# Softmax row sums in half as many matmuls, the first x tiles transposed by TensorE, and four PSUM banks for the first dense layer, in a gated mix of recurrent attention and an MLP

## The chip, the cores and the metric

The kernel runs on 1 core of one Trainium2 chip. The metric is the device time of one execution in microseconds (us); the figure of a kernel is the median of its runs. A granted TensorE clock of 1 means full speed.

## The reference

x is 2048 tokens of 512 numbers in bfloat16. The result is `g * a + (1 - g) * b`, with a gate g of one number per token.

```
g = sigmoid((x * gate_w).sum(-1, keepdims=True))
# a: recurrent attention, 64 segments of 32 tokens, M = 8 memory rows, 32 heads of 128
for s in range(n_seg):
    h = concatenate([mem, xs], axis=1)                 # 40 rows of 512
    q, k, v = h Wq, h Wk, h Wv                         # per head
    scores = where(mask, q k^T * Dh ** -0.5, -1e9)     # memory rows see all; tokens are causal
    p = softmax(scores, axis=-1)
    o = (p v) summed over heads through Wo
    mem = o[:, :M]                                     # goes into the next segment
    outs.append(o[:, M:])
# b: a token-wise MLP, F = 1376
y = (x - mean) / sqrt(var + 1e-5)
b = gelu(y w1 + b1) w2 + b2
```

The memory makes the 64 segments a chain: segment s+1 needs the eight memory rows that segment s put out.

## The kernel before

**Order of the work.** All of it stands in an order written out by hand (a manual schedule): each engine runs its instructions in the order in which the Python code issues them, and waits at each for its inputs and for its output tile to be free. There are no planner and no priorities. The eight PSUM banks are fixed: U[0] to U[3], X1, X2, SbF and W, all of 512 float32 columns.

**Start and MLP stage.** SyncE (SP) issues most loads, ScalarE (ACT) x tile 1 and the first piece of w2, GpSimd (POOL) the bias b1 and the broadcast of gate_w (L344). Eleven matmuls on the identity (`warm`, L524 to 528) run on TensorE (PE) while the first x tiles land. The 16 tiles of 128 tokens are worked off in 8 blocks of two. `prep` normalises a block's tiles on VectorE (DVE), `prep_tr` (L455) transposes them by PE through X1 and X2. `a_mm` (L477) is the first dense layer: for each of 11 chunks fc of the hidden size, four matmuls of 256 columns into a bank, then a Gelu on ScalarE (L483) that empties the bank. The bank (L480) goes by turns through SbF and W in blocks 1 to 6; the first four chunks of all and the last block use others. `b_mm` (L485) is the second dense layer for the same block, two chunks behind, into U[0] to U[3]. For nine of the tiles (DEF) it is put off: their hidden values go to DRAM (`spill`), and the loop computes them later in halves of four 256-column matmuls into W (`mlp_halves`, L667), one `next(mlp)` each, with the values fetched back by SP (`hm_load`). `gate_sums` (L462) multiplies x by gate_w on VectorE, and `gates` (L467) takes the tanh on ScalarE. At block 3, SP loads tiles 0 and 1 of x in transposed form (`load_xT`, L100, from L358) for the recurrent loop.

**One step of the loop** (L753 to 866, s from 0 to 63; each is one segment, T and si are its tile of 128 tokens and its place in it). Small matmuls are laid out four at a time in the PE array's four 32-wide column groups (`tile_position`), one per group of heads. In order:

- Q and K: 64 matmuls of 512 columns into U[0], U[2], U[1], U[3] (`qk_unit`, L125); ScalarE casts each bank to Tb (L133), VectorE transposes Tb into QT or KT (L137).
- `scores(s, 0)` (L261): 16 matmuls of 40 columns and four of 64, on top of a mask in SbF, for heads 0 to 15. The columns of a group of four heads are 8 left-over token keys' queries, then 32 queries (8 to 40), then two pieces of 8 for the memory rows (40 to 48, and 48 to 56 for the left-over keys), 56 in all (EW). ScalarE takes the exponential into E (L805).
- V: `v_unit(X1, ...)` four times, and one of the four for X2 (L147). ScalarE casts to V (L811).
- Sums over keys for heads 0 to 15, by matmuls with a block matrix of ones BO. `xsums` (L697) makes those of the 32 token columns: eight matmuls (four for columns 8 to 40, four for 0 to 8 that add to them), E as the weights, four columns of BO moving, into SbF[:, 224:232]. `msum` (L796, by `sums`, L275) makes those of the memory rows: four matmuls of 32 columns into U[1][:, 320:352], then four more that add the left-over keys' columns. `mnorm` (L799): VectorE takes the reciprocal (L801) from U[1] into SbF[:, 288:320], then multiplies it into E (L802).
- `scores(s, 1)` in U[0] for heads 16 to 31, two exponentials (first the memory columns 40 to 56, then the rest), two more V units.
- One MLP half, then `msum(1)` into U[3] and `mnorm(1)` through the SBUF tile RS; the last V unit, two V casts.
- Fill work (left-over tokens of the next tile and the like), one MLP half, `xsums(E, 1)`, and `recip_x` (L710): reciprocal of the 8 columns of sums into R; R to DRAM (r_dr, 4 KB) and back, broadcast to all partitions as Rb (512 KB), both by SP; copies of the memory rows' reciprocals into R; the mask written afresh into SbF with zeros for the next sums (`mask_put`, L257); POOL adds R into racc.
- `av` (L283): E times V, in two halves i2 = 0 and 1, into U[0] to U[3]; the memory columns of E are normalised by now, the token columns aren't. ScalarE casts the memory columns to UT (L842), the raw token columns to XR (L707).
- The output projection `wo_pass` (L732) into X2 with UT, which holds this step's memory rows and the token rows of step s-1; casts to w; `new_mem` (L740) puts the eight memory rows into the next step's input hT, by PE and VectorE.
- `x_norm(s)` (L725) runs on POOL at the start of step s+1: it multiplies XR by Rb, which arranges the reciprocals by head and query, into the next UT and into UL (L730, four instructions).

racc and rmin gather all reciprocals; at the end they decide whether a slower, safe version of the attention (tc.If) has to run. It doesn't here.

Of the kernel before, what the change touches and what calls it, by code (L numbers as in the profile page):

```python
# [28 lines left out]
def kernel(ctx, tc, A_x, A_mem0, A_Wq, A_Wk, A_Wv, A_Wo, A_seg_len, B_x, B_w1, B_b1, B_w2, B_b2, gate_w, out):  # L29
# [50 lines left out]

    MkF = ep.tile([P, 4 * EW + NG + 2 * M], BF16)
    Mk = MkF[:, 0:4 * EW].rearrange("p (a c) -> p a c", c=EW)
# [170 lines left out]
    RS = ep.tile([P, 32], FP32)  # L253
    RP = [SbF[:, 288:320], RS[:]]


    def mask_put(i2):  # L257
        c = 4 * EW + (NG + 2 * M if i2 == 0 else 0)
        nc.vector.tensor_copy(out=(SbF, U[0])[i2][:, 0:c], in_=MkF[:, 0:c])
# [41 lines left out]
    with tc.tile_pool(name="mlpw", bufs=1) as mlpw, \  # L301
# [129 lines left out]
        def prep(blk):  # L431
# [3 lines left out]
            for tt in range(TB):  # L435
# [3 lines left out]
                if blk == 0:  # L439
                    nc.vector.tensor_scalar(out=ve[:, tt:tt + 1], in0=mv[:, tt, 1:2], scalar1=LN_EPS, scalar2=None, op0=ALU.add)  # L440
                    nc.scalar.activation(out=rs[:, tt:tt + 1], in_=ve[:, tt:tt + 1], func=ACTF.Sqrt)
            if blk == 0:
                nc.scalar.activation(out=dummy[:], in_=ident[:, 0:1], func=ACTF.Gelu_apprx_tanh)
            else:
                nc.vector.tensor_scalar(out=ve[:], in0=mv[:, :, 1], scalar1=LN_EPS, scalar2=1.0 / (RSQRT_K * RSQRT_K), op0=ALU.add, op1=ALU.mult)
                rsqrt(rs[:], ve[:], TB)
# [80 lines left out]

        warm(NWARM)
        prep(0)
# [66 lines left out]
    UL = [cw.tile([P, 4, NG, 32], BF16, tag=f"UL{i}", bufs=1, name=f"UL{i}") for i in range(2)]  # L596
    racc = lp.tile([P, NG * 40], FP32)
    rmin = lp.tile([P, NG * 40], FP32)
# [93 lines left out]

    xs8 = SbF[:, 4 * EW:4 * EW + NG]
    xs8z = SbF[:, 4 * EW + NG:4 * EW + NG + 2 * M]
    RW = 9 * NG

    def xsums(E, h):  # L697

        for c0, n in ((8, 32), (0, LEFT)):
            for c in range(4):  # L700
                nc.tensor.matmul(xs8[32 * c:32 * c + n, 4 * h:4 * h + 4], lhsT=E[:, 4 * h + c, c0:c0 + n], rhs=BO[:, 0:P:32],  # L701
                                 start=False, stop=True, skip_group_check=True, tile_position=(0, 32 * c))

# [6 lines left out]
    def recip_x(s):  # L710
        R = Rs.pop(s)
        nc.vector.reciprocal(out=R[:, 8 * NG:RW], in_=xs8)
# [12 lines left out]
    def x_norm(s):  # L725
        T, si = divmod(s, SPT)
        XR, Rb = XRs.pop(s), Rbs.pop(s)[:].rearrange("p (c q) (h j) -> p h j c q", c=4, h=2)
        for out, o, a, b in ((UT[(s + 1) % 2], M, LEFT, 32), (UL[T % 2], LEFT * si, 0, LEFT)):
            for h in range(2):
                nc.gpsimd.tensor_tensor(out=out[:, :, 4 * h:4 * h + 4, o:o + b - a], in0=XR[:, :, 4 * h:4 * h + 4, a:b], in1=Rb[:, h, :, :, a:b], op=ALU.mult)  # L730

# [21 lines left out]
    for s in range(nseg):  # L753
# [42 lines left out]
        def msum(i2):  # L796
            sums(U[1 + 2 * i2][:, 320:352].rearrange("p (i q) -> p i q", q=8), E[:, 4 * i2:4 * i2 + 4, :], 40, 48, 8, True)

        def mnorm(i2):  # L799
            r, e = RP[i2], E[:, 4 * i2:4 * i2 + 4, 40:56].rearrange("p i (a q) -> p i a q", q=8)  # L800
            nc.vector.reciprocal(out=r, in_=U[1 + 2 * i2][:, 320:352])  # L801
            nc.vector.tensor_tensor(out=e, in0=e, in1=r.rearrange("p (i q) -> p i q", q=8).unsqueeze(2).to_broadcast([P, 4, 2, 8]), op=ALU.mult)  # L802
# [22 lines left out]
        if not last:  # L825
            if s:
                next(mlp, None)
            msum(1)
# [231 lines left out]
```

## Time and profile before

| | before |
|---|---|
| median of 3 runs | 751.95 us (751.55 to 753.9) |
| the profiled execution | 755.67 us, its span 753.8 us |
| granted TensorE clock | 0.998 |
| PE busy | 736.0 us (98%), 19896 matmuls |
| ACT busy | 535.6 us (71%) |
| DVE busy | 399.5 us (53%) |
| POOL busy | 274.2 us (36%) |
| DMA traffic | 77.17 MB, of which Rb 63 times 512 KB |
| last first-layer matmuls | from 68.75 us |
| Q and K of step 0 | from 74.58 us |

The profile is one execution, taken by the hardware. Names are those of the program with buffer numbers left out, so U stands for U[0] to U[3] and X for X1 and X2. A row of a group gives the line, the engine, the operation, `out<-in` and the count; then the busy time in us and the mean of one in ns; then the idle time just before them and who ended it. A row of the timeline starts with its start and duration in us, and shows in brackets the idle time before it and who ended that. "x8" in it are eight instructions in one row; its duration is from the first one's start to the last one's modelled end. Matmuls are pipelined, so ends overlap: what PE spends on a row is the distance to the start of the next one. "issue" is time in which an engine waited for nothing that the profile shows. A step of the loop takes some 10.5 us (the multiply from RS comes 63 times from 80.9 to 730.4).

### The profile page before, as it was taken

The numbers are of one execution on the slowest core, as the hardware profiler recorded it, in microseconds if no ns is written. First come the engines' busy times: TensorE is split into PE (matmuls) and PEld (weight loads), VectorE is DVE, ScalarE is ACT, GpSimd is POOL, SyncE is SP. The second block draws the span as 40 slices with busy tenths as digits, with TensorE's granted clock in tenths as the row PEclk, the third lists the DMA queues.
The fourth block names the chain that finished last, engine by engine and source line by source line (L and its number), as shares of the span: only waits on it lengthen the run. The fifth ranks groups of instructions, "written<-read, shape, count | busy, mean of one in ns | idle before, by whom it ended". The sixth has DMA issues, their size and how long they took to land.

```text
span 753.8 us, 45384 instructions
## 1 busy us (share of the span) xinstructions
PE 736.0 (98%) x19896; PEld 429.8 (57%) x19896; DVE 399.5 (53%) x1415; ACT 535.6 (71%) x1627; POOL 274.2 (36%) x516
## 2 busy tenths in 40 slices
PE   8999999999999999999999999999999999999996
PEld 5776555555555555555555565555555655555553
DVE  6776555446454554445554545445464545555444
ACT  5777667777776776777777777767777777777663
POOL 4001323444324444334433344333443334433341
PEclk9999999999999999999999999999999999999999
DMA  9999323122321323221322313231323222222321
GB/s 312 343 335 362 104 85 87 55 76 72 93 77 46 91 70 96 69 83 53 92 77 80 86 46 93 68 96 67 70 72 86 79 72 78 57 90 74 95 70 37
DMA packets 69997, 77.17 MB, mean 102 GB/s; under 512 B 34873, under 2 KB 59938, under 8 KB 68258
## 3 DMA queue, kind: packets, MB, share of 16 engines
q1 hardware_dynamic: 68802, 72.65, 31.4%
q8 instruction: 157, 2.57, 1.4%
q0 software_dynamic: 448, 1.05, 0.5%
q10 hardware_dynamic: 544, 0.52, 0.3%
q14 instruction: 46, 0.38, 0.2%
HBM read 60.21 MB, written 7.70 MB: 90 GB/s over the span
## 4 chain that ended last, share of the span: by engine, by line
PE 91%; DVE 3%; DMA 2%; issue 2%; ACT 1%; POOL 0%; DVEq 0%; SPq 0%; ACTq 0%; POOLq 0%
PE U L128 33%; PE X L159 19%; PE X L147 17%; PE X L128 4%; PE U L290 3%; PE W L674 3%; PE U L147 2%; PE SbF L482 1%; PE U L266 1%; DMA xt<-in_A_x_dram 1%; PE W L482 1%; PE U L489 1%; DVE junk L465 1%; PE SbF L266 1%; PE SbF L701 1%
## 5 line engine op out<-in xcount | busy, mean ns | idle before, releaser
L730 POOL TENSOR_TENSOR UT<-XR,Rb 128x384 bf16<-128x384 bf16 x126 | 140.2, 1134 | 310.1 <-DMA Rb<-r_dr 252.6
L133 ACT CAST Tb<-U 128x512 bf16<-128x512 f32 x288 | 168.7, 586 | 78.7 <-PE U L128 72.5
L128 PEld LDWEIGHTS <-hT 128*32 128x32 bf16 x4096 | 108.9, 96 | 95.5 <-DVE hT L748 1.1
L147 PE MATMUL X<-Wv_sb,hT 128*32 128x512 bf16 x2048 | 144.9, 378 | 0.9 <-issue 0.9
L128 PE MATMUL U<-Wq_sb,hT 128*32 128x512 bf16 x2048 | 145.1, 380 | 0.0
L128 PE MATMUL U<-Wk_sb,hT 128*32 128x512 bf16 x2048 | 144.6, 379 | 0.0
L159 PE MATMUL X<-Wo_sb,UT 128*32 128x512 bf16 x2016 | 123.0, 380 | 0.2
L748 DVE CAST hT<-U 128x8 bf16<-128x8 f32 x126 | 21.0, 167 | 172.0 <-PE U L746 131.1
L811 ACT CAST V<-X 128x256 bf16<-128x256 f32 x256 | 88.7, 372 | 16.4 <-PE X L147 3.5
L137 DVE STREAM_TRANSPOSE QT<-Tb 128x256 f32<-128x256 f32 x128 | 57.0, 446 | 71.9 <-ACT Tb L133 71.5
L159 PEld LDWEIGHTS <-UT 128*32 128x32 bf16 x2048 | 56.6, 96 | 57.1 <-issue 17.7
L707 ACT CAST XR<-U 128x256 bf16<-128x256 f32 x252 | 78.6, 438 | 0.0
L737 ACT CAST w<-X 128x128 bf16<-128x128 f32 x189 | 44.8, 310 | 45.8 <-PE X L159 45.1
L137 DVE STREAM_TRANSPOSE KT<-Tb 128x256 f32<-128x256 f32 x128 | 57.0, 445 | 25.3 <-ACT Tb L133 25.3
L730 POOL TENSOR_TENSOR UL<-XR,Rb 128x128 bf16<-128x128 bf16 x126 | 60.2, 500 | 0.0
L147 PEld LDWEIGHTS <-hT 128*32 128x32 bf16 x2048 | 47.0, 94 | 22.3 <-issue 1.8
L842 ACT CAST UT<-U 128x64 bf16<-128x64 f32 x252 | 35.3, 227 | 28.2 <-PE U L295 28.2
L722 POOL TENSOR_TENSOR racc<-racc,R 128x72 f32<-128x72 f32 x63 | 21.2, 337 | 93.6 <-DVE R L720 49.9
L674 PE MATMUL W<-w_sb,hm 128*32 128x256 bf16 x728 | 52.7, 273 | 0.1
L794 ACT ACTIVATE E<-U 128x64 bf16<-128x64 f32 (+1 forms) x128 | 35.0, 273 | 11.3 <-PE U L270 11.1
L482 PEld LDWEIGHTS <-w_sb 128*128 128x128 bf16 (+1 forms) x352 | 33.5, 100 | 13.4 <-issue 2.4
L159 PE MATMUL X<-Wo_sb,UL 128*32 128x512 bf16 x512 | 39.8, 379 | 0.2 <-issue 0.2
(178 smaller groups left out, 1223.0 us busy)
## 6 DMA issues: line engine op xcount, KB each, us to landing
Rb<-r_dr SPq DMA_DIRECT2D x63, 512.0 KB, 3.9
Wv_sb<-in_A_Wv_dram SPq DMA_DIRECT2D x4, 1024.0 KB, 7.2
Wq_sb<-in_A_Wq_dram SPq DMA_DIRECT2D x4, 1024.0 KB, 8.5
Wk_sb<-in_A_Wk_dram SPq DMA_DIRECT2D x4, 1024.0 KB, 9.0
Wo_sb<-in_A_Wo_dram SPq DMA_DIRECT2D x4, 1024.0 KB, 9.7
VP<-VL SPq DMA_DIRECT2D x64, 64.0 KB, 3.2
hm<-h_dr SPq DMA_DIRECT2D x91, 32.0 KB, 2.2
c<-c_dr SPq DMA_DIRECT2D x16, 128.0 KB, 3.5
```

The source lines that it names most:

```text
L128: nc.tensor.matmul(bk[32 * j:32 * j + 32, :], lhsT=G[:, kc, :], rhs=W5[t][:, kc, h0:h1, j, :], start=(kc == 0), stop=(kc == KC - 1), tile_ ...
L133: nc.scalar.copy(out=Tb[:], in_=bk.rearrange("p (a b e) -> p a e b", a=8, b=2))
L137: nc.vector.transpose(out=dst[:, 8 * hf:8 * hf + 8, c0:c0 + 32, :].rearrange("p a r b -> p a (r b)").bitcast(FP32), in_=Tb[:].rearrange("p ...
L147: nc.tensor.matmul(bk[32 * j:32 * j + 32, :], lhsT=G[:, kc, :], rhs=Wv5[:, kc, 4 * vb:4 * vb + 4, j, :], start=(kc == 0), stop=(kc == KC - ...
L159: nc.tensor.matmul(bk[32 * c:32 * c + 32, :], lhsT=U_[:, j, i, :], rhs=Wo_sb[:, 4 * i + j, :], start=(n == 0), stop=(n == NW - 1), tile_po ...
L482: nc.tensor.matmul(hp[:rows, 0:TB * P], lhsT=w1_sb[:, kc, fc * P:fc * P + rows], rhs=yTs[blk][:, kc, :], start=(kc == 0), stop=(kc == KC - 1))
L674: nc.tensor.matmul(W[32 * c:32 * c + 32, cc], lhsT=hm[:, 32 * c:32 * c + 32], rhs=w2_sb[:, fc, cc], start=(fc == 0 and h == 0), stop=(fc = ...
L707: nc.scalar.copy(out=XR[:, j], in_=U[j][:, 0:NG * 40].rearrange("p (i q) -> p i q", q=40)[:, :, 0:32])
L730: nc.gpsimd.tensor_tensor(out=out[:, :, 4 * h:4 * h + 4, o:o + b - a], in0=XR[:, :, 4 * h:4 * h + 4, a:b], in1=Rb[:, h, :, :, a:b], op=ALU ...
L737: nc.scalar.copy(out=w[:, a:b], in_=bk[:, a:b])
L811: nc.scalar.copy(out=V[:, i0:i0 + 2, :].rearrange("p i e -> p (i e)"), in_=(X1, X2)[vb][:, 256 * h:256 * h + 256])
L842: nc.scalar.copy(out=UT[s % 2][:, j, :, 0:M], in_=U[j][:, 0:NG * 40].rearrange("p (i q) -> p i q", q=40)[:, :, 32:40])
```

## The change

Five edits.

1. **Sums.** `xsums` takes four matmuls for eight: BO's columns are the weights, and E's 40 columns move, so that a sum for every query column (8 left-over and 32) lies along the columns, 48 of them reserved per half (XQ) in SbF[:, 224:320]. `msum` takes four for eight: 64 columns at once, the left-over keys' in columns of their own. What PSUM added up before is added by VectorE: a `tensor_reduce` of pairs (64 to 32 per partition) in each `mnorm`, ahead of a reciprocal that now works in place (in SbF or RS), and one of 16 pairs in `recip_x`. `recip_x` takes 64 reciprocals per partition for 8; only every eighth partition's go to r_dr, whose 16 rows of 64 are broadcast as before; `x_norm` reads Rb with a stride of one element along the queries where it was eight. R, racc and rmin are 128 wide there for 72, `mask_put(0)` is 336 wide for 248.
2. **Place of an MLP half.** The half ahead of `msum(1)` moves ahead of `scores(s, 1)`.
3. **Banks.** `a_mm` goes through SbF, W, U[1] and U[3] in turn, in every block.
4. **First x tiles.** Tiles 0 and 1 of x in transposed form come from eight PE transposes among the warm matmuls (one fewer of those) and two ScalarE copies, in place of two transposing DMAs of SP at block 3.
5. **gate_w.** Its broadcast moves from POOL's queue to SP's, behind two more pieces of w2.

```diff
-    r_dr = [dram.tile([P, NG], FP32, name=f"r_dr{i}") for i in range(2)]
+    r_dr = [dram.tile([16, 8 * NG], FP32, name=f"r_dr{i}") for i in range(2)]
...
-        nc.gpsimd.dma_start(gw_bc[:], gate_w.partition_broadcast(P))
         ld_w2(nc.sync, H2, H2 + 2)
         ld_w2(nc.sync, H2 + 2, FC - 1)
+        nc.sync.dma_start(gw_bc[:], gate_w.partition_broadcast(P))
...
             if blk == 3:
-                for T in range(2):
-                    load_xT(T)
...
-            hp = (SbF, W, U[3], SbF)[n] if n < 4 else (W, SbF, U[2], U[3])[n % 4] if blk == NBLK - 1 else (W, SbF)[n % 2]
+            hp = (SbF, W, U[1], U[3])[n % 4]
...
-        warm(NWARM)
+        def xp(T):
+            tp = U[T][:].bitcast(BF16)[:, 0:Dm].rearrange("p (k t) -> p k t", k=KC)
+            for kc in range(KC):
+                nc.tensor.transpose(tp[:, kc, :], xts[T][:, kc * P:(kc + 1) * P], ident[:])
+
+        def xp_out(T):
+            xTs[T] = ew.tile([P, KC, P], BF16, tag="xT", bufs=3, name="xT")
+            nc.scalar.copy(out=xTs[T][:], in_=U[T][:].bitcast(BF16)[:, 0:Dm].rearrange("p (k t) -> p k t", k=KC))
+
+        warm(NWARM - 6)
+        xp(0)
+        warm(2)
+        xp(1)
+        warm(3)
...
     def xsums(E, h):
-        for c0, n in ((8, 32), (0, LEFT)):
-            for c in range(4):
-                nc.tensor.matmul(xs8[32 * c:32 * c + n, 4 * h:4 * h + 4], lhsT=E[:, 4 * h + c, c0:c0 + n], rhs=BO[:, 0:P:32],
-                                 start=False, stop=True, skip_group_check=True, tile_position=(0, 32 * c))
+        for c in range(4):
+            nc.tensor.matmul(xs[32 * c:32 * c + 32, h, 0:40], lhsT=BO[:, 0:P:4], rhs=E[:, 4 * h + c, 0:40],
+                             start=False, stop=True, skip_group_check=True, tile_position=(0, 32 * c))
...
-        nc.vector.reciprocal(out=R[:, 8 * NG:RW], in_=xs8)
-        Rb = cw.tile([P, P, NG], FP32, tag="Rb", bufs=1, name="Rb")
-        nc.sync.dma_start(r_dr[s % 2][:], R[:, 8 * NG:RW])
+        nc.vector.tensor_reduce(out=xs[:, :, 40:48], in_=xs[:, :, 0:16].rearrange("p h (a q) -> p h q a", a=2), axis=AX.X, op=ALU.add)
+        nc.vector.reciprocal(out=R[:, 8 * NG:RW].rearrange("p (h q) -> p h q", h=2), in_=xs[:, :, 16:48])
+        Rb = cw.tile([P, 16, 8 * NG], FP32, tag="Rb", bufs=1, name="Rb")
+        nc.sync.dma_start(r_dr[s % 2][:], R[0:P:8, 8 * NG:RW])
...
-                nc.gpsimd.tensor_tensor(out=out[:, :, 4 * h:4 * h + 4, o:o + b - a], in0=XR[:, :, 4 * h:4 * h + 4, a:b], in1=Rb[:, h, :, :, a:b], op=ALU.mult)
+                nc.gpsimd.tensor_tensor(out=out[:, :, 4 * h:4 * h + 4, o:o + b - a], in0=XR[:, :, 4 * h:4 * h + 4, a:b], in1=Rb[:, h, :, :, r:r + b - a], op=ALU.mult)
...
         def msum(i2):
-            sums(U[1 + 2 * i2][:, 320:352].rearrange("p (i q) -> p i q", q=8), E[:, 4 * i2:4 * i2 + 4, :], 40, 48, 8, True)
+            for j in range(4):
+                nc.tensor.matmul(U[1 + 2 * i2][32 * j:32 * j + 32, 320:384], lhsT=BO[:, 32 * j:32 * j + 32], rhs=E[:, 4 * i2:4 * i2 + 4, 40:56],
+                                 start=True, stop=True, skip_group_check=True, tile_position=(0, 32 * j))
...
-            nc.vector.reciprocal(out=r, in_=U[1 + 2 * i2][:, 320:352])
+            m = U[1 + 2 * i2][:, 320:384].rearrange("p (i a q) -> p i q a", i=4, a=2)
+            nc.vector.tensor_reduce(out=r.rearrange("p (i q) -> p i q", q=8), in_=m, axis=AX.X, op=ALU.add)
+            nc.vector.reciprocal(out=r, in_=r)
...
             mnorm(0)
+            if s:
+                next(mlp, None)
         scores(s, 1)
...
-            if s:
-                next(mlp, None)
             msum(1)
```

The instructions of VectorE in one step of the loop, from the last KT transpose to the mask for the next step, first before (U_119 is U[1], U_121 is U[3], MkF the mask, an output's shape stands at the end):

```order
L137 STREAM_TRANSPOSE KT<-Tb 128x256
L801 RECIPROCAL SbF<-U_119 128x32
L802 TENSOR_TENSOR E<-E,SbF 128x4x16
L801 RECIPROCAL RS<-U_121 128x32
L802 TENSOR_TENSOR E<-E,RS 128x4x16
L712 RECIPROCAL R<-SbF 128x8
L720 COPY R<-RS 128x32
L720 COPY R<-SbF 128x32
L259 CAST SbF<-MkF 128x248
```

And the same stretch of VectorE in the changed kernel:

```order
L138 STREAM_TRANSPOSE KT<-Tb 128x256
L819 TENSOR_REDUCE SbF<-U_119 128x32
L820 RECIPROCAL SbF<-SbF 128x32
L821 TENSOR_TENSOR E<-E,SbF 128x4x16
L819 TENSOR_REDUCE RS<-U_121 128x32
L820 RECIPROCAL RS<-RS 128x32
L821 TENSOR_TENSOR E<-E,RS 128x4x16
L726 TENSOR_REDUCE SbF<-SbF 128x2x8
L727 RECIPROCAL R<-SbF 128x64
L735 COPY R<-RS 128x32
L735 COPY R<-SbF 128x32
L260 CAST SbF<-MkF 128x336
```

Three reduces have come in, one ahead of each reciprocal, and the reciprocals of `mnorm` read what the reduce wrote, not PSUM bank U.

On TensorE before, the MLP half (hm) stands between the second and third X2 units of V and `msum(1)` (X_123 is X2, hT the step's input); the last two rows of what precedes it, the half's last two, and the first of the sums:

```order
L147 LDWEIGHTS hT_88
L147 MATMUL X_123<-Wv_sb,hT_88 32x512
L674 LDWEIGHTS hm
L674 MATMUL W<-w_sb,hm 32x256
...
L277 LDWEIGHTS BO
L277 MATMUL U_121<-E,BO 32x32
```

In the changed kernel the half stands on TensorE between `msum(0)` and `scores(s, 1)` (U_118 is U[0]):

```order
L715 MATMUL SbF<-E,BO 32x40
L813 LDWEIGHTS BO
L813 MATMUL U_119<-E,BO 32x64
...
L689 LDWEIGHTS hm
L689 MATMUL W<-w_sb,hm 32x256
...
L267 LDWEIGHTS KT
L267 MATMUL U_118<-QT,KT 32x40
```

and behind the third X2 unit of V `msum(1)` follows at once:

```order
L148 LDWEIGHTS hT_87
L148 MATMUL X_123<-Wv_sb,hT_87 32x512
L813 LDWEIGHTS BO
L813 MATMUL U_121<-E,BO 32x64
```

So the four matmuls of the half have left the place between the second exponential's scores and its sums, and stand ahead of those scores; the sums themselves are four matmuls for eight in each place.

More of the change, by code (lines that the diff above doesn't have):

```diff
@@ L253 @@
     RS = ep.tile([P, 32], FP32)
-    RP = [SbF[:, 288:320], RS[:]]
+    RP = [SbF[:, 336:368], RS[:]]
     def mask_put(i2):
-        c = 4 * EW + (NG + 2 * M if i2 == 0 else 0)
+        c = 4 * EW + (2 * XQ + 2 * M if i2 == 0 else 0)
         nc.vector.tensor_copy(out=(SbF, U[0])[i2][:, 0:c], in_=MkF[:, 0:c])
@@ L726, in x_norm @@
         T, si = divmod(s, SPT)
-        XR, Rb = XRs.pop(s), Rbs.pop(s)[:].rearrange("p (c q) (h j) -> p h j c q", c=4, h=2)
-        for out, o, a, b in ((UT[(s + 1) % 2], M, LEFT, 32), (UL[T % 2], LEFT * si, 0, LEFT)):
+        XR, Rb = XRs.pop(s), Rbs.pop(s)[:].rearrange("p (c j) (h q) -> p h j c q", c=4, h=2)
+        for out, o, a, b, r in ((UT[(s + 1) % 2], M, LEFT, 32, 0), (UL[T % 2], LEFT * si, 0, LEFT, 32 - LEFT)):
             for h in range(2):
-                nc.gpsimd.tensor_tensor(out=out[:, :, 4 * h:4 * h + 4, o:o + b - a], in0=XR[:, :, 4 * h:4 * h + 4, a:b], in1=Rb[:, h, :, :, a:b], op=ALU.mult)
+                nc.gpsimd.tensor_tensor(out=out[:, :, 4 * h:4 * h + 4, o:o + b - a], in0=XR[:, :, 4 * h:4 * h + 4, a:b], in1=Rb[:, h, :, :, r:r + b - a], op=ALU.mult)
     def wo_pass(U_, cuts=(0, Dm), bk=W):
```

14 lines of the change are left out of this document (9 added, 5 removed).

## The prediction

> **What bounds the kernel now.** I read the page's busy shares and chain first, then one step of the recurrent loop on the timeline, engine by engine.
>
> ```profile
> PE 736.0 (98%) x19896; PEld 429.8 (57%) x19896; DVE 399.5 (53%) x1415; ACT 535.6 (71%) x1627; POOL 274.2 (36%) x516
> ...
> PE 91%; DVE 3%; DMA 2%; issue 2%; ACT 1%; POOL 0%; DVEq 0%; SPq 0%; ACTq 0%; POOLq 0%
> ```
>
> PE is 98% busy and 91% of the chain. So a matmul taken away could be worth its time, but only where nothing else already holds PE at the same place. Here is PE in step s=22, from the exponential sums to the end of the attention-times-V matmuls (start, duration, instruction; the pitch from one row's start to the next is what PE spends):
>
> ```profile
> 311.24 0.20 PE L701 MATMUL SbF<-BO,E 128*32 128x4 bf16 x8
> 311.30 0.18 PE L277 MATMUL U<-E,BO 128*32 128x32 bf16 x4
> ...
> 311.37 0.28 PE L266 MATMUL U<-QT,KT 128*32 128x40 bf16 x16
> 311.49 0.20 PE L270 MATMUL U<-QT,KL 128*32 128x64 bf16 x4
> 311.52 0.61 PE L147 MATMUL X<-Wv_sb,hT 128*32 128x512 bf16 x8
> 311.95 0.29 PE L674 MATMUL W<-w_sb,hm 128*32 128x256 bf16 x4
> 312.07 0.20 PE L277 MATMUL U<-E,BO 128*32 128x32 bf16 x4
> ...
> 312.12 0.40 PE L147 MATMUL X<-Wv_sb,hT 128*32 128x512 bf16 x4
> ...
> 312.76 0.29 PE L674 MATMUL W<-w_sb,hm 128*32 128x256 bf16 x4
> 312.88 0.22 PE L701 MATMUL SbF<-BO,E 128*32 128x4 bf16 x8
> 313.02 0.28 PE L290 MATMUL U<-E,V 32*128 32x40 bf16 x16
> ...
> 313.17 0.32 PE L290 MATMUL U<-E,V 32*128 32x40 bf16 x16
> ...
> 313.45 0.61 PE L159 MATMUL X<-Wo_sb,UL 128*32 128x512 bf16 x8
> ```
>
> and VectorE, then ScalarE, beside it:
>
> ```profile
> 310.87 0.45 DVE L137 STREAM_TRANSPOSE KT<-Tb 128x256 f32<-128x256 f32 x1 [0.38 <-ACT Tb L133]
> 311.66 0.37 DVE L801 RECIPROCAL SbF<-U 128x32 f32<-128x32 f32 x1 [0.34 <-ACT V L811]
> 312.06 0.22 DVE L802 TENSOR_TENSOR E<-E,SbF 128x64 bf16<-128x64 bf16 x1
> 312.35 0.36 DVE L801 RECIPROCAL RS<-U 128x32 f32<-128x32 f32 x1
> 312.81 0.23 DVE L802 TENSOR_TENSOR E<-E,RS 128x64 bf16<-128x64 bf16 x1
> 313.25 0.21 DVE L712 RECIPROCAL R<-SbF 128x8 f32<-128x8 f32 x1 [0.21 <-PE SbF L701]
> 313.38 0.13 DVE L720 COPY R<-RS 128x32 f32<-128x32 f32 x1
> ```
> ```profile
> 311.79 0.22 ACT L794 ACTIVATE E<-U 128x64 bf16<-128x64 f32 x1 [0.17 <-PE U L270]
> ...
> 312.56 0.65 ACT L811 CAST V<-X 128x256 bf16<-128x256 f32 x2
> ```
>
> Three hidden holds show. (a) scores(1), at 311.37, starts 0.05 after the KT transpose ends (310.87+0.45=311.32): however early the sums ahead of it finish, it cannot start sooner. (b) msum(1), at 312.07, starts 0.06 after the exponential it sums (311.79+0.22=312.01), that is 0.70 after scores(1) began; the deferred-MLP half at 311.95 just fills this wait. (c) The second half of av starts at 313.17; the normalised E it reads is ready at 312.81+0.23=313.04, 0.13 earlier. The V casts end at 312.56+0.65=313.21, inside it. So here PE runs with 0.1 us or less to spare on three sides.
>
> **The sums.** Eight 4-column matmuls take 0.06, the pair of four 32-column ones 0.07 with the wait for KT in it, sixteen 40-column ones (L266) 0.12 and four 64-column ones (L270) 0.03: small matmuls cost about 7 ns each, whatever their width. Sixteen fewer are worth 16 x 7 = 0.11 us per step, 7 us over 63 steps, if nothing holds PE.
>
> **The moved MLP half.** After the change xsums(0) takes 0.03, msum(0) 0.03 and the half 0.12 or a little less (312.76 to 312.88), so scores(1) starts near 311.41, 0.04 later than now. msum(1) follows 0.70 later, at 312.11 (hold b), but its cover is now only the eight V matmuls (0.43), done at 311.41+0.15+0.43=311.99: PE idles 0.12 there. Behind it on PE stand four V matmuls, the fill, the second sums and av. The saving in front and the lost cover cancel.
>
> **The normalisation.** Each mnorm gets a tensor_reduce ahead of the reciprocal, in series on VectorE. The trace has no reduction of 64 PSUM values to 32. The nearest rows:
>
> ```profile
> L884 DVE TENSOR_REDUCE tot<-R 128x1 f32<-128x256 f32 x1 | 0.4, 414 | 0.0
> ...
> L748 DVE CAST hT<-U 128x8 bf16<-128x8 f32 x126 | 21.0, 167 | 172.0 <-PE U L746 131.1 <-ACT w L737 36.3
> ```
>
> Between them lies 1 ns per element: 167 + 56 = 0.22 for 64 elements. The ends are 0.17 and 0.41; I stay by the PSUM row, which is nearer in size. Now the chain. The first reduce starts when the sums reach VectorE: today 0.29 after the next PE work starts (311.37 to 311.66), so at 311.30+0.28=311.58. Reduce to 311.80, reciprocal 311.83 to 312.20 (0.03 between dependent operations, as from 311.66+0.37 to 312.06), multiply 312.23 to 312.45. An independent operation may start 0.08 before that ends (313.38 against 313.25+0.21): 312.37. The second sums are ready at the same time: 312.11, +0.03 for msum, +0.23 (312.12 to 312.35). Second reduce to 312.59, reciprocal 312.62 to 312.97, multiply 0.10 later (as now), 313.07 to 313.30, PE at 313.35. PE itself would arrive at 312.14 + 0.64 + 0.12 + 0.12 (second sums with four fewer) + 0.15 = 313.17. It waits 0.18, and av ends at 313.35+0.28-0.04 = 313.59 (the 0.04 being the V-cast wait now inside that half) against 313.45. **Loss 0.14 us in each of 62 steps: 8.7 us**; what is queued behind, the whole output projection, moves with it. With the reduce at 0.17 the second one is held by PE alone, and the loss is 0.09 (5.6 us); at 0.41 both reduces count, 0.52 (32 us).
>
> That a late multiply is paid one for one is in the trace. In step s=3 it took 0.67 and held av:
>
> ```profile
> 113.58 0.67 DVE L802 TENSOR_TENSOR E<-E,RS 128x64 bf16<-128x64 bf16 x1
> ```
> ```profile
> 114.30 0.28 PE L290 MATMUL U<-E,V 32*128 32x40 bf16 x16 [0.20 <-DVE E L802]
> ```
>
> **The cross-row sums.** recip_x gets a reduce (0.20) and 64 reciprocals for 8 (6.2 ns each from the 32- and 8-wide rows: 0.56 for 0.21), after a multiply 0.26 later: R is ready 0.62 later than 313.46. A longer step gives back 0.14, so Rb and x_norm come about 0.5 later in the next one. PE needs x_norm's result only in the output pass, so the path is covered; mask_put's extra columns run behind recip_x, ahead of new_mem, which waits for that output pass. The cost is on VectorE: the multiply from RS waits when x_norm runs beside it.
>
> ```profile
> L802 DVE TENSOR_TENSOR E<-E,RS x63: 225/226/667, 80.9 to 730.4; 128x64 bf16<-128x64 bf16 x63
> ```
> ```profile
> L730 POOL TENSOR_TENSOR UT<-XR,Rb 128x384 bf16<-128x384 bf16 x126 | 140.2, 1134 | 310.1 <-DMA Rb<-r_dr 252.6 <-ACT Tb L133 50.4 <-ACT E L805 7.0
> L730 POOL TENSOR_TENSOR UL<-XR,Rb 128x128 bf16<-128x128 bf16 x126 | 60.2, 500 | 0.0
> ```
>
> Those waits cost a few steps up to 0.44 now. With x_norm 0.5 later and the multiply 0.26 later they grow a little if POOL keeps its pace: 0 to +1.5 us. Rb's inner stride falls from 8 floats to 1, and if POOL gains from that they shrink: down to -1.5. I take 0. [...]
>
> **First dense layer.** In blocks 1 to 6 PE waits once for a bank:
>
> ```profile
> 17.98 0.38 PE L489 MATMUL U<-w_sb,hTm 128*128 128x512 bf16 x1
> 18.50 0.60 PE L482 MATMUL SbF<-yT,w_sb 128*128 128x256 bf16 x4
> ```
> ```profile
> 57.77 0.38 PE L489 MATMUL U<-w_sb,hTm 128*128 128x512 bf16 x1
> 58.27 0.60 PE L482 MATMUL W<-yT,w_sb 128*128 128x256 bf16 x4
> ```
> ```profile
> 17.98 0.47 ACT L483 ACTIVATE hTm<-SbF,b_sb 128x256 bf16<-128x256 f32 x1
> ```
>
> A 512-column matmul is worth 0.22; the rows take 0.52 and 0.50, the first and last of six. The start at 18.50 is 0.05 after the Gelu that frees the bank (17.98+0.47). With four banks that Gelu is needed only after the next 0.44 of matmuls. Gain 6 x 0.29 = 1.75 us.
>
> **Start, x tiles, gate_w.** Ten warm matmuls (11 took 4.87) and eight transposes end some 0.4 later than eleven did:
>
> ```profile
> 1.47 4.87 PE L526 MATMUL U<-ident 128*128 128x512 bf16 x11 [1.47 <-POOL ident masks.py:199]
> ```
> ```profile
> PEld L482 <- DMA w_sb<-in_B_w_dram: 0.7, 1, 0.7
> ```
>
> The second row, a wait in the first block for w1's last piece, swallows it: cost 0, or 0.4 without that cover. gate_w leaving POOL takes 128 KB from ahead of that piece, and two transposing DMAs leave a saturated queue: 0 to -0.8, I take -0.2. gate_w lands later on SP's queue; VectorE's gate sums and then ScalarE's tanh queue behind it, with the four banks as cover.
>
> **Irregular waits.**
>
> ```profile
> PE U L290 <- issue: 3.2, 5, 1.0
> ```
>
> A new 0.18 wait just ahead lets instruction supply catch up: 0 to -0.9, I take -0.5.
>
> **Sum.** +8.7 - 1.75 - 0.2 - 0.5 = +6.25 us. The profiled execution (755.67, span 753.8) would become 761.9; it lies 3.7 above the median of the three runs, so from 751.95 the forecast is 758.2.
>
> **Rivals.** (1) *Normalisation hidden; the other side.* If the second half of av can start by about 313.20, PE or the V casts bound it as today and the recurrent loop stays near +0.02 per step (+1.2). This takes a VectorE chain 0.15 shorter, say an in-place reciprocal that is far quicker from SBUF than the 0.36 from PSUM. For it: no row has that reciprocal at 32 elements. Against: 8, 32 columns scale by the element. With the other terms at their good ends, 1.2-1.75-0.8-0.9-1.5 = -3.7: 748.2. (2) *Cheap reduce.* At 0.17, with the same good ends, 5.6-4.95 = +0.7: 752.6. (3) *Dear reduce*, 0.28 or more: both reduces then sit in the chain, 0.14+0.06+0.06=0.26, 16 us; 765 and up. For it: the strided PSUM read pairs values 8 apart, which no row shows. (4) *gate_w late*: a stall of ScalarE of up to 1 us, 759. (5) *The matmul count decides*, nothing holds PE: -7 -2.45, 742.5; hold (a) alone speaks against it.
>
> **How the numbers follow.** Forecast band, 754.3 to 763: 0.54, with (4) inside. (3): 0.17. (2): 0.15. (1) 0.11 and (5) 0.03. A measurement of this kernel tells about 0.3% (2.3 us) from no change; so faster 0.14, same 0.15, slower 0.71. The range, 751 to 766, leaves out (1), (5) and the dear end of (3).
>
> **What would show it.** In the new profile: the two reduces at 0.22 each; av's second half starting 0.05 after the multiply from RS, at a wait of about 0.18; msum(1) 0.05 after its exponential with an idle PE before it; the six bank waits gone; x_norm's rows shorter or not. Wrong if the reduces take under 0.15, or if the multiply ends before PE arrives.

## The result, and the profile after

The changed kernel takes 755.38 us (median of 10 runs, 754.14 to 756.36) beside 752.02 us for the kernel before; the ratio is 1.0051, with a 95% interval of 1.0035 to 1.0067, so 2.6 to 5.0 us slower. The forecast was 758.2 us, slower, in a range of 751 to 766. The sign came out, and so did the mechanism, a wait of TensorE at av. But two losses were put too low and one gain far too low; these errors partly cancelled, so that the number came out as near as it did is in part luck.

The profiled execution of after (755.33 us, span 753.5) lies at its median, that of before (755.67 us) 3.6 us above its own. The two spans are thus nearly alike and must not be subtracted. The first line of the page after:

```profile
PE 736.9 (98%) x18895; PEld 419.2 (56%) x18895; DVE 457.5 (61%) x1604; ACT 536.5 (71%) x1629; POOL 246.4 (33%) x515
```

TensorE has 1001 matmuls fewer in the record and is as busy as before; VectorE is busy for 58 us more. One step, s=23, on TensorE and then on VectorE, as in the prediction (start, duration, instruction):

```profile
319.15 0.19 PE L715 MATMUL SbF<-E,BO 128*32 128x40 bf16 x4
319.18 0.20 PE L813 MATMUL U<-E,BO 128*32 128x64 bf16 x4
319.21 0.28 PE L689 MATMUL W<-w_sb,hm 128*32 128x256 bf16 x4
319.32 0.27 PE L267 MATMUL U<-QT,KT 128*32 128x40 bf16 x16
...
320.01 0.21 PE L813 MATMUL U<-E,BO 128*32 128x64 bf16 x4
...
320.81 0.21 PE L715 MATMUL SbF<-E,BO 128*32 128x40 bf16 x4
320.95 0.27 PE L291 MATMUL U<-E,V 32*128 32x40 bf16 x16
321.06 0.19 PE L296 MATMUL U<-E,VP 32*128 32x64 bf16 x4
321.29 0.28 PE L291 MATMUL U<-E,V 32*128 32x40 bf16 x16
```
```profile
319.50 0.23 DVE L819 TENSOR_REDUCE SbF<-U 128x32 f32<-128x64 f32 x1 [0.27 <-PE W L689]
319.77 0.37 DVE L820 RECIPROCAL SbF<-SbF 128x32 f32<-128x32 f32 x1
320.17 0.22 DVE L821 TENSOR_TENSOR E<-E,SbF 128x64 bf16<-128x64 bf16 x1
320.30 0.22 DVE L819 TENSOR_REDUCE RS<-U 128x32 f32<-128x64 f32 x1
320.55 0.35 DVE L820 RECIPROCAL RS<-RS 128x32 f32<-128x32 f32 x1
321.01 0.23 DVE L821 TENSOR_TENSOR E<-E,RS 128x64 bf16<-128x64 bf16 x1
```

The second multiply ends at 321.24, the second half of av starts 0.05 later, and TensorE had been free since about 321.09 (four matmuls of 7 ns behind 321.06): it waits 0.20 there. From the first sums to the output fill behind av it is 2.38 (319.15 to 321.53) against 2.21 before.

The list of TensorE's waits has changed too (each row: who waited for whom, the total in us, how many times, the longest). It has no "issue" row any more, where before had five. The row for the second multiply was small before and is now the largest of the list; here it is first in before, then in after:

```profile
PE U L290 <- DVE E L802: 0.4, 2, 0.2
```
```profile
PE U L291 <- DVE E L821: 4.1, 15, 0.6
```

### The profile page after: what moved, and what is told of

It reads as the page before. It is cut to its first block, busy times and chain, and to the rows that moved or that the text cites. A ratio compares the mean times of both kernels' runs of the same rounds, so it can differ in the third digit from the quotient of the medians.

```text
span 753.5 us, 43569 instructions
## 1 busy us (share of the span) xinstructions
PE 736.9 (98%) x18895; PEld 419.2 (56%) x18895; DVE 457.5 (61%) x1604; ACT 536.5 (71%) x1629; POOL 246.4 (33%) x515
## 5 line engine op out<-in xcount | busy, mean ns | idle before, releaser
L745 POOL TENSOR_TENSOR UT<-XR,Rb 128x384 bf16<-128x384 bf16 x126 | 114.2, 927 | 320.7 <-DMA Rb<-r_dr 256.2
L129 PEld LDWEIGHTS <-hT 128*32 128x32 bf16 x4096 | 107.6, 96 | 96.9 <-DVE hT L763 1.0
L148 PE MATMUL X<-Wv_sb,hT 128*32 128x512 bf16 x2048 | 142.7, 378 | 0.0
L160 PE MATMUL X<-Wo_sb,UT 128*32 128x512 bf16 x2016 | 120.4, 380 | 0.0
L737 POOL TENSOR_TENSOR racc<-racc,R 128x128 f32<-128x128 f32 x63 | 28.8, 457 | 113.8 <-DVE R L735 109.1
L148 PEld LDWEIGHTS <-hT 128*32 128x32 bf16 x2048 | 45.2, 95 | 20.9 <-issue 0.3
L689 PE MATMUL W<-w_sb,hm 128*32 128x256 bf16 x728 | 50.9, 272 | 1.0 <-DMA hm<-h_dr 0.7
L745 POOL TENSOR_TENSOR UL<-XR,Rb 128x128 bf16<-128x128 bf16 x126 | 51.4, 429 | 0.0
L291 PE MATMUL U<-E,V 32*128 32x40 bf16 x2048 | 35.0, 177 | 6.5 <-DVE E L821 4.1
```

The lines of the kernel that those rows point to most:

```text
L129: nc.tensor.matmul(bk[32 * j:32 * j + 32, :], lhsT=G[:, kc, :], rhs=W5[t][:, kc, h0:h1, j, :], start=(kc == 0), stop=(kc == KC - 1), tile_ ...
L148: nc.tensor.matmul(bk[32 * j:32 * j + 32, :], lhsT=G[:, kc, :], rhs=Wv5[:, kc, 4 * vb:4 * vb + 4, j, :], start=(kc == 0), stop=(kc == KC - ...
L160: nc.tensor.matmul(bk[32 * c:32 * c + 32, :], lhsT=U_[:, j, i, :], rhs=Wo_sb[:, 4 * i + j, :], start=(n == 0), stop=(n == NW - 1), tile_po ...
L291: nc.tensor.matmul(Uv[j][:, i, :], lhsT=V[q, i, :], rhs=E[q, i, 8:48], start=(i == 0), stop=False, skip_group_check=True, tile_position=(3 ...
L689: nc.tensor.matmul(W[32 * c:32 * c + 32, cc], lhsT=hm[:, 32 * c:32 * c + 32], rhs=w2_sb[:, fc, cc], start=(fc == 0 and h == 0), stop=(fc = ...
```

## Experiments

All times are in us. "Beside" is the median of the kernel before that was run with the kernel; it differs between such groups (750.92 to 754.63), so kernels of different groups are compared by their ratio. "Step" is the shortest of the steps s=10, 14, ... 54 (the same place in each tile, so the same work), from the first matmul of scores(s,0) to that of the next step: a step without stops. "Refill stops" are explained under e1; they belong to the profiled execution, whose time stands behind them.

| kernel | sum matmuls, wait at av | median | beside | ratio (95%) | step | refill stops (time) |
|---|---|---|---|---|---|---|
| before | 32, no | 752.02 | | | 10.172 | 10.1 (755.67) |
| e1 before again | 32, no | 751.04 | 752.03 | | 10.166 | 6.5 (751.04) |
| e2 first stage only | 32, no | 747.67 | 752.03 | 0.9947 (0.9928 to 0.9967) | 10.169 | 8.3 (750.03) |
| e3 late multiply | 32, yes | 757.67 | 752.03 | 1.0083 (1.0062 to 1.0104) | 10.298 | 5.7 (757.81) |
| after | 16, yes | 755.38 | 752.02 | 1.0051 (1.0035 to 1.0067) | 10.346 | 1.5 (755.33) |
| e4 after, 16 idle matmuls | 32, yes | 758.73 | 752.03 | 1.0101 (1.0079 to 1.0123) | 10.346 | 2.2 (757.26) |
| e5 after, half back | 16, yes | 757.45 | 754.63 | 1.0043 (1.0024 to 1.0062) | 10.346 | 0.7 (755.91) |
| e6 old memory sums | 24, no | 754.54 | 754.63 | 1.0009 (0.9988 to 1.0031) | 10.195 | 8.7 (754.31) |
| e7 the same, half back | 24, no | 752.60 | 754.63 | 0.9965 (0.9943 to 0.9987) | 10.150 | 11.0 (755.98) |
| e8 second sums old | 20, no | 748.98 | 754.63 | 0.9923 (0.9894 to 0.9952) | 10.170 | 6.2 (748.26) |
| e9 the same, half back | 20, no | 747.92 | 750.92 | 0.9952 (0.9932 to 0.9972) | 10.150 | 4.7 (745.38) |
| e10 after, fill ahead | 16, moved | 757.98 | 750.92 | 1.0099 (1.0076 to 1.0123) | 10.361 | 1.7 (758.05) |
| e11 after again | 16, yes | 755.46 | 750.92 | 1.0059 (1.0038 to 1.0080) | 10.349 | 1.9 (755.29) |
| e12 few sums, no reduce | 16, no | 744.91 | 754.13 | 0.9875 (0.9856 to 0.9894) | 10.127 | 4.6 (744.94) |

There are two theories. **The chain**: VectorE's longer normalisation holds the second half of av, as predicted. **The supply**: TensorE loses time in the loop when its instructions are not there yet, and the change takes most of that away. Rivals stand in the expectations.

**e1, the kernel before once more** (no edit).

> The kernel before, unchanged, for a second profile. Supply theory: TensorE loses 5 to 11 us of the loop in stops with nothing to wait for, that end 1.2 to 1.6 us after a 16 KB packet of the instruction queue has landed; a step without such a stop takes 10.17 to 10.46 us as in the first profile. Rival (outlier): the stops belong to the one slow profiled execution (755.67 us); another one near 752 us has less than 2 us of them, and its loop is longer than 10.3 us per step for another reason.

One execution, 751.04 us. The stops are there again, about as many but shorter. The clearest one of the first profile is in step s=40, in the middle of the 16 equal matmuls of a half of av:

```profile
500.35 0.19 PE L295 MATMUL U<-E,VP 32*128 32x64 bf16 x4
500.37 0.29 PE L290 MATMUL U<-E,V 32*128 32x40 bf16 x10
501.67 0.22 PE L290 MATMUL U<-E,V 32*128 32x40 bf16 x6 [1.00 <-issue]
```

All 16 read the same tiles, E and V, and the last writes of these had ended by 500.42 (the V casts) and 500.25 (the multiply); so no data was late for the last six alone. The DMA view for the microsecond ahead of it (499.2 to 500.2) has one packet of the instruction queue:

```profile
q8 instruction: 1, 0.02, 5.8%
```

It is 16 KB, started at 499.26 and took 0.92; TensorE went on 1.49 after its end. The other stops of this kind in before end 1.2 to 1.5 after such a packet too (92.88 to 93.42 after 91.93; 207.40 to 208.26 after 206.94; 323.49 to 324.25 after 322.90). The page's rows of the queue for the whole run, before and after:

```profile
q8 instruction: 157, 2.57, 1.4%
```
```profile
q8 instruction: 149, 2.44, 1.3%
```

There is a packet for every 256 instructions of TensorE's program, weight loads counted (255.9 on average between the starts in before and 255.7 in after, by the program's order). I call such a packet a refill and the 256 instructions a block. In the stop shown, TensorE went on 0.92 + 1.49 = 2.4 us after the refill's start. Ten of the larger stops begin 1.1 to 2.0 after the start of a refill, when TensorE stands about half way through a block (116 to 176 instructions in). Half a block is no fixed limit: in eight other blocks of before TensorE came 185 to 232 instructions far by 1.2 after the packet's end without such a stop, and what decides it stays open. At 7 ns for a small matmul with its weight load TensorE gets that far soonest in the dense part of the step, around the sums and av; the stops lie there and in the longer matmuls too.

Most of the 157 refills of before show no stop; some 20 of them do.

I count as refill stop each group of matmuls that is over 0.06 longer than its kind usually is (a quarter of the kind is shorter than that), if its longest gap ended 1.1 to 1.8 after a packet, a third to seven tenths of a block into the next one: 21 of them, 6.5 us, in e1, and 22, 10.1 us, in the first profile. The difference, 3.6 us, is most of the 4.6 between these two executions. The outlier rival falls.

This count chooses by the time since a packet and does not ask what ended the gap. A count that does the reverse takes every distance between two neighbouring matmuls of the loop that is over 0.22 longer than usual at that place and was ended by "issue". All 14 profiles have 128 of these, and 123 end 1.1 to 1.8 after a packet, though in the loop packets come 4.4 (before) to 4.7 (after) apart on average. That ties the stops to the refills by their timing; no run moved the refills themselves. The 123 come to these sums per profile:

| 32 sum matmuls, no wait | 24, no wait | 20, no wait | 16, no wait | 32, wait | 16, wait |
|---|---|---|---|---|---|
| before 10.8, e1 7.3, e2 7.7 | e6 9.4, e7 11.5 | e8 2.2, e9 2.7 | e12 2.4 | e3 5.8, e4 1.2 | after 0, e5 0.3, e10 1.1, e11 0.7 |

**e2, the first stage alone** (edits 3, 4 and 5; the loop is that of before).

> The kernel before with edits 3, 4 and 5 alone (four banks, x tiles by TensorE, gate_w by SyncE). All theories: 1.75 + 0.2 less in the first stage, 750.0 us, with the loop as before. Supply theory: the stops in the loop stay (5 us or more). If the profile of after is read rightly (loop begins 2.1 us earlier), 749.9.

747.67 us, 4 us faster and not 2. In the trace the loop's first scores begin at 76.40 (before 78.03 and 78.61): 1.6 to 2.2 of it. The six bank waits are gone, as in the trace of after: a 512-column matmul is followed 0.21 later, where it was 0.52.

```profile
17.42 0.38 PE L490 MATMUL U<-w_sb,hTm 128*128 128x512 bf16 x1
17.63 0.60 PE L483 MATMUL U<-yT,w_sb 128*128 128x256 bf16 x4
```

The rest must lie in the loop, whose program is that of before; the profiled execution (750.03, slower than the median) has 8.3 us of stops and does not show why. Left open.

**e3, before with a later second multiply.**

```diff
         nc.vector.reciprocal(out=r, in_=U[1 + 2 * i2][:, 320:352])
+            if i2 == 1:
+                nc.vector.reciprocal(out=r[:, 0:8], in_=U[3][:, 320:328])
```

> The kernel before with one more reciprocal of 8 columns (about 0.24 us with its gap) ahead of the second multiply, matmuls unchanged: TensorE should wait about 0.16 at the second half of av, as in the kernel after. No supply theory: +0.14 to +0.17 in each of 62 steps, 760.5 to 762.5 us. Supply theory: the wait lets refills catch up, so 4 to 8 us of stops go: 754 to 758 us. Of the two forms of the supply theory: if the wait alone does it, nearly all stops go (754); if the number of instructions counts as well, half stay (757).

757.67, 5.6 us slower. The step is 0.13 longer; over 63 steps that is 8.2 us, and refill stops fell to 5.7. The hold works as in after, though the matmuls are those of before (the second half of av starts 0.05 after the multiply ends):

```profile
324.65 0.23 DVE L804 TENSOR_TENSOR E<-E,RS 128x64 bf16<-128x64 bf16 x1
324.71 0.19 PE L295 MATMUL U<-E,VP 32*128 32x64 bf16 x4
324.93 0.28 PE L290 MATMUL U<-E,V 32*128 32x40 bf16 x16
```

The time grew by less than the steps did, so the wait gave part of itself back; that refills arrive meanwhile fits, and is not shown directly.

**e4, after with 16 idle matmuls per step.**

```diff
+        for _ in range(4):
+            for j in range(4):
+                nc.tensor.matmul(U[3][32 * j:32 * j + 32, 384:448], lhsT=BO[:, 32 * j:32 * j + 32], rhs=BO[:, 0:64],
+                                 start=True, stop=True, skip_group_check=True, tile_position=(0, 32 * j))
         xsums(E, 1)
```

> The kernel after with 16 idle matmuls of 64 columns (ones times ones into unused PSUM columns) ahead of the second token sums, which brings the loop back to the number of matmuls of before; 16 x 7 ns = 0.11 us per step lie inside TensorE's wait of 0.2 ahead of the second half of av. Supply theory, number of instructions: stops come back, 3 to 8 us, 758.5 to 763 us. Supply theory, wait alone, and no supply theory: 755.4 to 756.5 us.

758.73, 3.4 above after, in the range for the number of instructions. But its profile (757.26, the shortest of its six runs) shows only 2.2 us of refill stops for 1.5, the same step, and 0.4 more ahead of the loop and 1.3 more behind it. The time speaks for the number of instructions, the stops (3 to 8 us expected) speak against it: inconclusive. e3 and e4 have the same number of matmuls and both have the wait, and yet 5.7 and 2.2 us of stops; so these two things alone do not set them.

**e5, after with the MLP half back** ahead of msum(1) (edit 2 undone).

> The kernel after with the MLP half back ahead of the second memory sums (edit 2 undone). Chain theory: the second multiply is late because of what VectorE runs before it, not because of when its sums come, so the loop stays within 0.01 us per step of after: 755.4 +- 1.5. Rival (lost cover): what after loses is the idle TensorE ahead of msum(1), 0.1 per step, and it comes back: 749 us or less.

The step is the same to the nanosecond, 10.346, and the ratio 1.0043. In its trace msum(1) starts 0.82 after the first sums (median of the steps), 0.04 earlier than in after, and the second half of av still starts 2.14 after them in both: the chain sets it, not when the sums come.

**e6 and e7, the memory sums of before in after**: `msum` by eight matmuls, no reduce in `mnorm`; in e7 the half is back too.

```diff
...
-            m = U[1 + 2 * i2][:, 320:384].rearrange("p (i a q) -> p i q a", i=4, a=2)
-            nc.vector.tensor_reduce(out=r.rearrange("p (i q) -> p i q", q=8), in_=m, axis=AX.X, op=ALU.add)
-            nc.vector.reciprocal(out=r, in_=r)
+            nc.vector.reciprocal(out=r, in_=U[1 + 2 * i2][:, 320:352])
```

> The kernel after with the memory sums and their normalisation of before (8 matmuls a time, reciprocal from PSUM, no reduce in mnorm); token sums, r_dr, Rb, first stage and the half's place as in after; 24 sum matmuls per step for 32 before and 16 after. Chain theory: the hold at the second half of av goes, a step without stops takes 10.14 to 10.17 (10.34 after), the time is that of the first stage alone (747.7) less 0 to 3 us: 744.5 to 747.5. Rival (the token sums' part costs: longer recip_x, mask, racc on VectorE and POOL): 750 or more.

> As e6, with the half back at its old place too. By the prediction's sum the saving ahead of scores(1) and the lost cover cancel: within 1.5 us of e6. Rival: the half's place decides where no chain holds; 0.1 per step, 6 us, either way.

The steps without stops came out as the chain says: 10.195 and 10.150 for 10.346, so the 0.15 to 0.20 that went was the memory sums' normalisation, and the longer recip_x, mask and racc cost such a step nothing. The times did not: 1.0009 and 0.9965 of before, where 744.5 to 747.5 us, about 0.990 to 0.994, had been expected. By its time alone e6 would bear out its rival (750 or more); against the rival stand its step, and e8, which keeps the same token sums and is 5.6 us faster. With no wait at av the stops are back, 8.7 and 11.0 us. Here the half's place counts, 0.045 per step, and e7 is 1.9 us below e6 where 1.5 at most had been expected: in e6 scores(1) starts 0.19 after the first sums, in e7 0.13, and msum(1) comes 0.68 to 0.69 after scores(1) in both. e7's profiled execution also has one wait of 2.2 for a DMA (hm, in s=3).

**e8 and e9, only the second memory sums as before**; the first keep their reduce. In e9 the half is back.

> The kernel after with only the second memory sums and their normalisation as before (no reduce in mnorm(1)); the first keep their reduce. Chain theory: the first reduce pushes the second reciprocal back by 0.04 to 0.05 us only, and TensorE does not arrive earlier at av: no hold, 743.5 to 747 us, within 1.5 us of e6. Rival: both reduces count alike, half of the 0.17 per step stays, 5 us above e6.

> As e8 (only the second memory sums as before, first with their reduce, token sums as after, first stage as after), with the MLP half back ahead of msum(1). In e6 and e7 the half's old place was worth 0.04 us per step where no reduce holds. If that carries over: 0.987 to 0.992 of before, some 2 us under e8. If the first reduce still sets the second reciprocal's start, no difference to e8: 0.990 to 0.995.

0.9923 and 0.9952 of before. e8 lies 5.6 us below e6 where 1.5 at most had been expected, and e9, expected at 0.995 or less, shows no gain over it. The step is that of e7 within 0.02, so the first reduce is hidden. The second multiply, and the second half of av behind it, in e8:

```profile
309.84 0.35 DVE L826 RECIPROCAL RS<-U 128x32 f32<-128x32 f32 x1
310.30 0.23 DVE L827 TENSOR_TENSOR E<-E,RS 128x64 bf16<-128x64 bf16 x1
310.46 0.27 PE L291 MATMUL U<-E,V 32*128 32x40 bf16 x16
310.58 0.20 PE L296 MATMUL U<-E,VP 32*128 32x64 bf16 x4
310.61 0.34 PE L291 MATMUL U<-E,V 32*128 32x40 bf16 x16
```

The multiply ends at 310.53 and av goes on at 310.61, straight behind its first half. Both versions beat the kernel before and after. They do not clearly beat e2, which has the same first stage and the loop of before (0.9947, interval 0.9928 to 0.9967): that the sums in them gain anything is not shown. e8's profiled execution has one wait of 2.5 for a DMA (hm, in s=3).

**e10, a fill unit of after moved ahead of av.**

```diff
-    WS = ((2, 2, 1), (2, 2, 2), (2, 2, 2), (2, 2, 2))
+    WS = ((3, 1, 1), (3, 1, 2), (3, 1, 2), (3, 1, 2))
```

> The kernel after with one more unit of fill work (four matmuls of 512 columns, 0.215 us) ahead of av and one less behind it (sums as after: 16 matmuls, three reduces). Hold theory: the unit fills TensorE's wait of 0.2 ahead of the second half of av; the shorter cover behind av costs about 0.1 at the first use of UT; a step without stops falls from 10.34 to 10.2 to 10.28. No supply theory: 0.993 to 0.999 of before. Supply theory, the hold had absorbed the stops: they come back from 1.5 us to 5 us or more in the loop, and the time stays at 1.000 to 1.005. Supply theory, fewer instructions had done it: stops stay under 3 us, 0.993 to 0.999.

A miss: 1.0099. The wait at av is filled, but the second half still starts 2.15 after the first sums (2.14 in after), and behind av the wait is back in full:

```profile
322.35 0.28 PE L291 MATMUL U<-E,V 32*128 32x40 bf16 x16
322.46 0.22 PE L296 MATMUL U<-E,VP 32*128 32x64 bf16 x4
322.61 0.40 PE L148 MATMUL X<-Wv_sb,GL 128*32 128x512 bf16 x4
322.73 0.56 ACT L861 CAST UT<-U 128x64 bf16<-128x64 f32 x4 [0.56 <-PE U L296]
323.09 0.40 PE L160 MATMUL X<-Wo_sb,UT 128*32 128x512 bf16 x4
```

wo_pass starts 0.48 after av ends, whatever lies between (0.46 before). From the sums to wo_pass the step is in this kernel, as in after, one chain of latencies through VectorE, av and the casts of UT; TensorE's fill work only hides it. As the wait only moved, the stops stayed low and the test didn't separate the two forms of the supply theory. Of the 2.5 us that it is slower than after (e11), the step explains 0.8 (63 x 0.012); the rest is not explained.

**e11, after once more** (no edit).

> The kernel after, unchanged, for a second profile on the chip of e9 and e10. Refill stops below 2.5 us again, a step without stops 10.34 to 10.63, 1.0035 to 1.0067 of before. If its stops are 5 us or more, the first profile of after was a lucky one and the supply theory has no case.

As expected: 1.0059, 1.9 us of refill stops.

**e12, 16 sums and no reduce**: the half at its old place.

```diff
-            m = U[1 + 2 * i2][:, 320:384].rearrange("p (i a q) -> p i q a", i=4, a=2)
-            nc.vector.tensor_reduce(out=r.rearrange("p (i q) -> p i q", q=8), in_=m, axis=AX.X, op=ALU.add)
-            nc.vector.reciprocal(out=r, in_=r)
+            m = U[1 + 2 * i2][:, 320:384].rearrange("p (i a q) -> p i a q", i=4, a=2)
+            nc.vector.reciprocal(out=r.rearrange("p (i q) -> p i q", q=8), in_=m[:, :, 0, :])
...
```

> The kernel after with the MLP half at its old place and without the reduce in mnorm: the reciprocal is taken from the main keys' memory sums alone, so the left-over keys' part is left out of the memory rows' normalisation. 16 sum matmuls per step as in after, but no reduce: the missing corner between before (32 sums, no hold: 10.1, 6.5 and 8.3 us of refill stops), e3 (32, hold: 5.7) and after (16, hold: 1.5 and 1.9). Chain theory: no wait ahead of the second half of av, a step without stops at 10.13 to 10.16. Stops absorbed by the hold: 5 us or more of them, 746 to 749 us. Stops removed by the number of instructions: under 3 us, 741 to 745 us.

744.91, 0.9875. The step is 10.127, the shortest of all, and the stops lie between the two answers: 4.6 us. But that count holds gaps that ended in the same window and were waits for data: at 679.39 one of 0.36 for the multiply, at 451.70 one of 0.38 for a DMA (VP). The count by "issue" gives 2.4; with it, as with the time, the test falls on the side of the number of instructions. Put beside the others, both forms of the supply theory hold a part. Without the wait: 6.5 to 10.1 (32 sums), 8.7 and 11.0 (24), 6.2 and 4.7 (20), 4.6 (16). With it: 5.7 and 2.2 (32), and 0.7 to 1.9 (16, three profiles). The table under e1 has the same order, with a step between 24 and 20. One profile for most, so the size is rough. A rival stays untested: every edit also shifts where the blocks begin in a step (601 recorded TensorE instructions per step with 32 sum matmuls, 585, 577 and 569 with 24, 20 and 16), and no run changed that alone.

## Why the forecast was right, point by point

**The hold at av** was there, at its place and for its reason. The reduces were put at 0.22 and took 0.23 and 0.22:

```profile
L819 DVE TENSOR_REDUCE SbF<-U 128x32 f32<-128x64 f32 x63 | 14.6, 232 | 17.5 <-PE U L813 8.8 <-PE W L689 8.1 <-PE U L271 0.6
L819 DVE TENSOR_REDUCE RS<-U 128x32 f32<-128x64 f32 x63 | 13.6, 215 | 0.0
```

The wait is 0.20 for a forecast 0.18. The term, +8.7, was mis-sized: the step grew by 0.174 instead of 0.14, so 63 x 0.174 = +11.0 us. Of the 0.03, most was in the chain: from the first sums to the end of av it ran 2.38 for a worked-out 2.35 (the first reduce 0.01 longer and 0.01 later, its gap to the reciprocal 0.04 for 0.03); wo_pass then started 0.01 later behind av (0.47 for 0.46, medians). That only the second reduce stands in the way was implied (the first moves the second's start by little), and e8 shows it. Rival (1) fell on its own condition: the in-place reciprocal takes 0.37 and 0.35, as good as the 0.37 and 0.36 from PSUM bank U.

**The moved half.** "The saving in front and the lost cover cancel": e5 shows no effect, but because the chain hides both. Where nothing holds, they don't quite cancel: 0.045 lost (e6 against e7), 0.02 (e8 against e9). Holds (a) and (b) are as described: in e5, e7 and e12 the sums ahead of scores(1) are fewer and it still starts 0.13 after them, and msum(1) comes 0.67 to 0.69 after scores(1) in every version.

**First stage and start**: -1.95 forecast, and the loop begins 2.1 to 2.7 earlier (75.93 in after for 78.03 and 78.61). By the medians these edits are worth 4.4 (e2, 2.5 to 5.4 by its interval); the difference is open. gate_w's rival (4) didn't come: in the first 76 us of after no wait of TensorE for ScalarE is listed.

**x_norm and the multiply**: taken as 0 within 1.5, an estimate of the author's. GpSimd did gain from the stride of one:

```profile
L745 POOL TENSOR_TENSOR UT<-XR,Rb 128x384 bf16<-128x384 bf16 x126 | 114.2, 927 | 320.7 <-DMA Rb<-r_dr 256.2 <-ACT Tb L134 58.3 <-ACT E L824 6.2
L745 POOL TENSOR_TENSOR UL<-XR,Rb 128x128 bf16<-128x128 bf16 x126 | 51.4, 429 | 0.0
```

(927-429)/256 = 1.95 ns per element for (1134-500)/256 = 2.48 with the stride of eight in before: 0.79 of it. The collisions did not shrink with it:

```profile
L821 DVE TENSOR_TENSOR E<-E,RS x63: 224/225/737, 79.0 to 730.4; 128x64 bf16<-128x64 bf16 x63
```

A collision is a multiply from RS that starts while an x_norm row runs on GpSimd: 14 of the 63 in before, of which 13 take 0.25 to 0.67, and 17 in after, of which 14 take 0.25 to 0.74; the others take 0.22 to 0.23, in both kernels. The longest is 0.74 for 0.67, and the wait list now names the multiply 15 times, 4.1 us. Most of it is time in which these 15 steps would have waited the common 0.2 anyhow; the groups that contain it are 3.7 us over their usual length in after, 2.0 in before. That is +1.7 (+1.9 by e11 and e1), a little outside the bound.

**The irregular waits are the step that failed.** The prediction had: "A new 0.18 wait just ahead lets instruction supply catch up: 0 to -0.9, I take -0.5". The direction was right and the size wrong by some ten times: refill stops went from 6.5 to 10.1 us down to 1.5 to 1.9. The bound came from one row of the wait list (L290, 3.2 us). It should have come from the loop: in before the steps s=10, 14, ... 54 have a shortest of 10.172 and a mean of 10.318. The same stops stood in the same list under other names, and partly under none:

```profile
PE X L147 <- issue: 1.3, 3, 0.7
PE X L128 <- issue: 0.8, 1, 0.8
PE U L295 <- issue: 0.4, 1, 0.4
PE X L159 <- issue: 0.2, 1, 0.2
```

The prediction gave the new wait as the only reason. It left out that the change itself takes 32 instructions a step out of the dense stretch, 16 matmuls with their weight loads; e12, which has no reduce and still fewer stops than before, points to this as well.

**The sum by what was measured**: +11.0 - 2.4 + 1.7 = +10.3 without the stops; the measured +2.6 to +5.0 leaves -5.3 to -7.7 for them, and their fall in the profiles, 4.6 to 8.6, covers that. So 758.2 was too high by 2.8 us, because the gain from the stops was missed by some 5 to 7 us and two losses by 4 together. With e2's -4.4 for the first stage in place of -2.4, the stops' part would be -3.3 to -5.7, and the two edits in the loop cost 7.7 us (755.38 - 747.67). That the stops cause the remaining gap is shown by the 2 x 2 of before, e3, e12 and after only in kind; what sets the number of stops in a given run, and why groups of runs of the same kernel differ by 3.7 us, is not settled.

## What to carry to other kernels

Before pricing an edit in a loop, compare the shortest and the mean step: the gap is time that no row of the waits may own, and an edit can give it back. An operation added to a chain of latencies cost its length less the slack there, even on an engine that is 53% busy: of two reduces of 0.22 to 0.23 the first was free, the second cost 0.17 us a step. The better version is then not the one with the fewest matmuls: with the first memory sums in four and the second in eight (e8, e9), the kernel is 0.5 to 0.8% faster than before. The first-stage edits alone give 0.5% (e2), so undoing the change in the loop altogether does about as well; test each part of a change by itself.

## What had not been expected of the hardware

By the timing of its stops (of 128 by "issue" in the 14 profiles, 123 end 1.1 to 1.8 us after a 16 KB packet), TensorE runs out of instructions in a straight line of code. Small matmuls go at 7 ns each with their weight load (sixteen of 40 columns in 0.12 us or less), and in the stop at 500.48 it stood half way through a block of 256 instructions (124 recorded ones in) until about 2.4 us after the start of the 16 KB refill. A single stop in the loop of before takes up to 1.2 us (that one, to 501.67), and in before they come to 0.9 to 1.3% of the time. With a wait of TensorE for data in the same stretch there are fewer of them: 5.7 us in e3 beside 6.5 to 10.1 in before, 1.5 and 1.9 in after beside 4.6 in e12.
